# Retention attention into a SwiGLU block: the first pair in blocks of 128 tokens, SyncE asking for the weights, and the last half rounding moved

## The chip, the cores and the metric

The kernel runs on one core of a Trainium2 chip. The metric is the device time of one execution in microseconds (us). Three runs of the kernel before have a median of 1016.34 us (1016.2 to 1020.21). The profile is of one further execution, which took 1014.62 us in all, with a recorded span of 1012.9 us.

## The reference

Retention attention over q, k and v (8 batches, 8 heads, 576 tokens, 64 wide, float32) feeds a feed-forward block on 4608 tokens of width 512. The weights come as float64: 512 x 1536 twice and 1536 x 512 once.

```
scores = scale * q @ k.T
ret    = scores * where(i >= j, gamma[head] ** (i - j), 0)
x      = (ret @ v), heads side by side          # 4608 x 512
g      = x @ w_gate
out    = (silu(g) * (x @ w_val)) @ w_out
```

## The kernel before, in words

**Attention.** Two heads of one batch are a pair; a batch has four pairs (HP = 4), and there are 32. A pair is worked in chunks of 64 tokens. q and k are turned so that the 64 features lie on partitions; TensorE makes the scores of each chunk with itself (`scores`), which are multiplied by a decay mask `near` (`masked`, `own`); the chunk's key-value sums (`new_states`) are chained into running states on VectorE (`pairs`, `odd`, `evens`); and the outputs are the chunk's own part (`own_values`) and the part from the states (`earlier_values`), added in one bank of PSUM and put into x by `to_x`. Keys are scaled by a column of the table `tab`, which is loaded from DRAM.

The pairs 0 to 3, the first 512 tokens, are special. They are turned by TensorE (`transposes`, L466) and copied out of PSUM; pairs 1 to 3 have q scaled by GpSimd beforehand (`scale_run`, L735), pair 0 has its output scaled on VectorE instead (L645). `tick(t, 0, HP)` does one step of this start: scores and states of pair t-1, values of pair t-2, transposes of pair t. Later pairs are turned by VectorE (L492).

**The feed-forward block.** The 4608 tokens go in tiles: a first of 512, then four of 1024. For the first tile, `up0(f, chunks)` makes one of 12 filters f of 128 columns: gate and value, each four chunks (one per pair of x) of 128x128 weights against 512 tokens, in two of the four banks A, B, C, E; then the silu on ScalarE (L856) and the product on VectorE (L857). `down0` multiplies by w_out afterwards. Filters 0 and 1 are begun with chunks 0 and 1 while pair 3 is still being worked (L853), and finished with chunks 2 and 3. Filter 2 and the gate of filter 3 are written as two halves of 256 tokens (L850).

**Weights.** They are loaded in 18 pieces of 1 MB (`load_w`; `order` gives the sequence, pieces 0 to 11 gate and value of two filters each, 12 to 17 w_out), into three raw slots that take turns and one extra for the piece with m = 3. Each piece is turned from float64 into float32 in two halves j: ScalarE splits the words (`split`, L389 and L390), VectorE puts them together (`rounding`, L406 and L407). The split of a piece's second half asks for the piece three places later, which needs the slot. Before, SP asks for the first five pieces and ScalarE's queue for the rest.

**Order.** The order on every engine is the order of the program text (`manual_schedule`); there is no scheduler. The list `plan` interleaves roundings (`round_until`), `up0`, `tick` and the loads of later pairs (`load`, `next_load`) for filters 2 to 11. SP issues the loads of pairs in program order; each DMA uses one of eight semaphores, so a DMA waits until the one eight before it has landed. `end_loads` issues small loads from GpSimd for the last 64 tokens of batch 0.

Of the kernel before, what the change touches and what calls it, by code (L numbers as in the profile page):

```python
# [17 lines left out]
ALU = mybir.AluOpType  # L18
# [4 lines left out]
def tables(gamma, scale, L):  # L23

    g, at = np.array(gamma), np.arange(L)
    lane = np.arange(2 * L)[:, None]
    both = lambda t: np.repeat(t, L, axis=0).reshape(-1, 2 * L, t.shape[1]).transpose(1, 0, 2).reshape(2 * L, -1)
    twice = lambda t: np.concatenate([t, t])
    half = [np.repeat(g.reshape(-1, 2), L, axis=1).T ** (lane % 32 + 32 * r) for r in range(2)]
    pieces = scale * np.stack(half, axis=2).reshape(2 * L, -1)
    runs = scale * (g[None, :, None] ** ((4 * lane[:, :, None] + np.arange(4)) % L)).reshape(2 * L, -1)
    parts = [twice((g[:, None] ** -at).T), twice((g[:, None] ** (L - at)).T),
             both(g[:, None] ** L), both(g[:, None] ** (2 * L)), pieces, runs, both(scale * g[:, None] ** at),
             both((scale * g[:, None] ** at).reshape(-1, 2, L)[:, ::-1].reshape(-1, L))]  # L40
    return np.concatenate(parts, axis=1).astype(np.float32)
# [90 lines left out]
def kernel(  # L132
# [32 lines left out]
    nc = tc.nc  # L165

    B, H, S, D = q.shape
# [79 lines left out]
    def scaled(i):  # L247

        return 0 < i < HP
# [4 lines left out]
    def load(i):  # L254
# [6 lines left out]
        if i < HP:  # L261
# [11 lines left out]
            for h in heads:  # L273
                queues[i % 2].dma_start(out=blocks(t)[:, h % 2], in_=v[b, h, 0:CW].rearrange("(c p) d -> p c d", p=P))
# [35 lines left out]
    NCOL = 6 * H + 4 * HP  # L310
    nc.sync.dma_start(out=tab[:, 0:NCOL], in_=decays[:, 0:NCOL])
    load(0)
    load(1)
    ident = const.tile([P, P], F32, name="ident")
    make_identity(nc, ident)
    nc.scalar.activation(out=io[:, 0:1], in_=ident[:, 0:1], func=AF.Silu)
    inv, key = tab[:, 0:H], tab[:, H : 2 * H]
    step = tab[:, 2 * H : 2 * H + 2 * HP]
    piece = tab[:, 2 * H + 2 * HP : 2 * H + 4 * HP]
    run = tab[:, 2 * H + 4 * HP : NCOL]  # L320
# [11 lines left out]
    even_heads, odd_heads = slice(0, H, 2), slice(1, H, 2)  # L332
    for rows in half:
        decay(slice(0, H), slice(0, H), rows)

    load(2)
    nc.sync.dma_start(out=tab[:, NCOL:], in_=decays[:, NCOL:])
    load(3)
# [13 lines left out]
    order = [0, 1, 2, 3, 4, 5, 6, 12, 7, 8, 13, 9, 10, 14, 11, 15, 16, 17]  # L352
# [6 lines left out]
    def load_w(m, parts=range(2)):  # L359

        i, queue = order[m], nc.sync if m < 5 else nc.scalar
        n = m - (m > RAWS)
        raw = rest[:, raw_at + n % RAWS * 2048 : raw_at + (n % RAWS + 1) * 2048].rearrange("p (c x) -> p c x", c=HP)
        if m == RAWS:
            raw = x_odd[:, :, TW // 2 :]
        raws[i] = raw.bitcast(I32)
        dst, src = raw.bitcast(I64), weights[i][0]
        if i < NUP:
            for cols in [ts(2 * f + n, D) for f in parts for n in range(2)] if m <= RAWS else [slice(0, 2 * P)]:
                queue.dma_start(out=dst[:, :, cols], in_=src[:, :, cols])  # L370
        else:
            queue.dma_start(out=dst.rearrange("p (f c) n -> p f (c n)", f=2), in_=src)
# [7 lines left out]
    def split(j):  # L380

        i, f = halves[j]
        bits = bits_of(i, f)
        top, ulp = [rest[:, part_at + 512 * (2 * n + j % 2) : part_at + 512 * (2 * n + j % 2 + 1)] for n in range(2)]
        blocks = lambda a: a.rearrange("p (c m) -> p c m", m=P)
        nc.scalar.activation(out=blocks(top), in_=bits[:, :, :, 1].bitcast(F32), func=AF.Prelu, scale=2.0 ** -112, alpha=2.0 ** 32)  # L389
        nc.scalar.activation(out=blocks(ulp.bitcast(I32)), in_=bits[:, :, :, 0].bitcast(U32), func=AF.Copy, scale=2.0 ** -29)  # L390
        parts[j] = top.bitcast(I32), ulp.bitcast(I32)
        m = j - 2 if 1 < j < 4 else j // 2
        if f and m != RAWS and m + RAWS + (m < RAWS) < len(order):
            if j == 3:
                held.append(lambda: load_w(m + RAWS + (m < RAWS)))
            else:
                load_w(m + RAWS + (m < RAWS))
# [13 lines left out]
    for f in range(2):  # L411
        for m in range(2):
            load_w(m, (f,))
# [30 lines left out]
    def vector(i):  # L444

        return i == 0

    def transposes(i):
# [6 lines left out]
        copy = nc.scalar.copy if i else nc.vector.tensor_copy  # L455
        if i < HP:

            mine = (bankC, bankE) if i + 1 == HP else (bankB, bankA)
            parts = [(kT, kn, mine[0]), (qT, qk, mine[1])]
            if i == 0:  # L460
                parts.reverse()

            def turn(t, src, bank):
                for c in range(NFULL):
                    to = bank[:, c : 4 * P : NFULL] if t is qT and scaled(i) else bank[:, ts(c, P)]
                    nc.tensor.transpose(to, src[:, ts(c, P)], ident)  # L466

            def put(t, _, bank):
                if i or t is qT:
                    copy(t[:, 0:CW], bank)  # L470
                else:
                    copy(t[:, 0 : CW // 2], bank[:, 0 : CW // 2])
                    nc.scalar.copy(t[:, CW // 2 : CW], bank[:, CW // 2 :])

            if i + 1 == HP:
                for part in parts:
                    turn(*part)
                pieces = [lambda part=part: put(*part) for part in parts]
            else:
                for part in parts:  # L480
                    turn(*part)
                    put(*part)
# [13 lines left out]
        def keys():  # L496
# [5 lines left out]
            for hl, rows, at in parts:  # L502
                scale = key[rows, 2 * p + hl : 2 * p + hl + 1]
                if vector(i) or 1 < i < HP:
                    (nc.vector if vector(i) else nc.gpsimd).tensor_scalar(out=at, in0=at, scalar1=scale, scalar2=None, op0=ALU.mult)
                else:
                    nc.scalar.activation(out=at, in_=at, func=AF.Copy, scale=scale)
# [3 lines left out]
        return [keys] + pieces  # L511
# [64 lines left out]
    def masked(i):  # L576
# [6 lines left out]
        def copies():  # L583
            (nc.vector.tensor_copy if vector(i + 1) else nc.scalar.copy)(out=even, in_=z[:, 0])
# [151 lines left out]

    def tick(t, lo=HP, hi=NP, spread=False, then=None):
        go_on(len(pieces))
        if hi == HP:

            def new_pair():
                scores(t - 1, True)
                new_states(t - 1)
                pieces.extend(masked(t - 1))
                go_on(3)

            scale_run(t + 1)
            if lo < t < hi:
                new_pair()
            if lo <= t - 2 < hi:  # L750
                own_values(t - 2)
            for f in transposes(t) if lo <= t < hi and t + 1 < HP else ():
                f()
            if lo <= t - 2 < hi:
                earlier_values(t - 2)
                if t == HP:
                    up0(0, range(2))
                to_x(t - 2)[0]()
            if t + 1 == HP:
                split(0)  # L760
                after = transposes(t)
                rounding(0)
                for f in after:
                    f()
            if t == HP:
                rounding(2)
                rounding(3, False)
                new_pair()
                while held:
                    held.pop()()  # L770
                split(4)
                up0(1, range(2))
            return
# [68 lines left out]
    def up0(f, chunks):  # L842

        pair = banks[2 * (f % 2) : 2 * (f % 2) + 2]
        for gv, bank in enumerate(pair):
            for c in chunks:
# [6 lines left out]
                nc.tensor.matmul(bank, w, xs[0][:, c, :], start=(c == 0), stop=(c == HP - 1))  # L853
# [573 lines left out]
    for t in range(HP + 2):  # L1427
        tick(t, 0, HP)

        if t == 3:  # L1430
            load(HP)
        for j in {3: (1,), 5: (4, 5)}.get(t, ()):
            rounding(j)
    for c in range(2, HP):
        for f in range(2):
            up0(f, [c])
    load(HP + 1)
    for to, heads in ((even_heads, odd_heads), (odd_heads, even_heads)):
        decay(heads, to, half[1])
    nc.gpsimd.tensor_copy(out=last_near, in_=near[:, even_heads])  # L1440
    end_loads()
# [16 lines left out]
    plan.insert(1, lambda: tick(HP, HP, FIRST))  # L1458
    tick_at = {2: 4, 3: 5, 5: 6, 7: 7, 10: 8, 11: 9}
    for f in range(2, NF):  # L1460
        round_until({4: 12, 6: 13, 8: 14, 9: 15, 10: 16, 11: 17}.get(f, f + 2))
        plan.append(lambda f=f: up0(f, range(HP)))
        if f + 2 == NF:
            plan.append(lambda: split(2 * len(order) - 2))
# [3 lines left out]
        if f - 1 in tick_at and f < 7:  # L1468
            plan.append(lambda t=tick_at[f - 1]: next_load(t))
# [101 lines left out]
```

## Time and profile before

| what | value |
|---|---|
| median of three runs | 1016.34 us (1016.2 to 1020.21) |
| the profiled execution's own time | 1014.62 us |
| its span | 1012.9 us |
| TensorE busy | 1001.2 us, 99% of the span |
| VectorE, ScalarE, GpSimd busy | 714.8, 286.6, 561.9 us |
| moved by DMA | 194.38 MB, 192 GB/s on average |
| first matmul of filter 0, of filter 2 (timeline) | 24.02 us, 40.96 us |
| first matmul of `down0` (timeline) | 121.81 us |

A busy share is an average over the whole span. The change touches only the part before about 125 us, so the timeline and the busy time of short stretches say more about it. Starts are microseconds from the span's start. A float32 matmul appears as two records (two passes), so x32 is sixteen matmuls. Where an engine was idle before a row, the bracket at its end gives the time and what ended it.

### The profile page before, as it was taken

How to read it: one execution, taken by the hardware profiler on the slowest of the kernel's cores; microseconds unless marked ns; L12 is line 12 of the kernel's file. 1: busy time of each engine (PE TensorE's matmuls, PEld its weight loads, DVE VectorE, ACT ScalarE, POOL GpSimd, SP SyncE). 2: the span in 40 equal slices, each digit the busy share in tenths (PEclk: the TensorE clock that was granted, in tenths of full speed). 3: DMA queues.
4: the chain of work that ended last, by engine and by line, in shares of the span. 5: the costliest groups of instructions: out<-in, count | busy, mean ns of one | idle time of the engine just before them, and what ended most of it. 6: DMA issues, size and time to landing. Idle time of an engine off the chain costs nothing.

```text
span 1012.9 us, 21320 instructions
## 1 busy us (share of the span) xinstructions
PE 1001.2 (99%) x8336; PEld 825.6 (82%) x8336; DVE 714.8 (71%) x1206; ACT 286.6 (28%) x636; POOL 561.9 (55%) x589
## 2 busy tenths in 40 slices
PE   6999999999999999999999999999999999999998
PEld 5655555888888888888888888888888888888887
DVE  4488888677875766977777678866575767566645
ACT  4475522132423312132422202233220012232110
POOL 3400358979475228575564157746672586566614
PEclk9999999999999999999999999999999999999999
DMA  9999976877587786757577776434454554445553
GB/s 243 261 274 264 206 230 229 236 221 213 142 235 204 221 234 205 186 154 200 179 202 206 197 180 218 154 133 159 161 173 141 154 189 147 148 156 180 181 159 102
DMA packets 278892, 194.38 MB, mean 192 GB/s; under 512 B 212552, under 2 KB 246088, under 8 KB 278792
## 3 DMA queue, kind: packets, MB, share of 16 engines
q1 hardware_dynamic: 251464, 94.70, 36.5%
q10 hardware_dynamic: 26688, 97.92, 29.4%
q8 instruction: 66, 1.08, 0.5%
q0 software_dynamic: 640, 0.39, 0.2%
q14 instruction: 34, 0.28, 0.1%
HBM read 154.04 MB, written 38.93 MB: 191 GB/s over the span
## 4 chain that ended last, share of the span: by engine, by line
PE 96%; DVE 2%; DMA 1%; SPq 0%; ACT 0%; issue 0%; ACTq 0%; DVEq 0%
PE bankB L1186 12%; PE bankC L1186 12%; PE bankA L1186 11%; PE bankE L1186 11%; PE bankB L1392 7%; PE bankE L1392 7%; PE bankC L1392 7%; PE bankA L1392 6%; PE outer L532 2%; PE bankE L853 2%; PE bankA L853 2%; PE inner L1186 2%; PE outer L1186 2%; PE bankB L853 2%; PE outer L559 2%; PE bankC L853 2%
## 5 line engine op out<-in xcount | busy, mean ns | idle before, releaser
L1042 POOL TENSOR_TENSOR rest<-rest 128x512 f32<-128x512 f32 (+1 forms) x139 | 148.0, 1076 | 160.1 <-DVE rest L1042 112.7
L1201 POOL TENSOR_TENSOR arena<-rest,io 128x256 f32<-128x256 f32 x168 | 123.9, 750 | 88.9 <-ACT io L1200 84.2
L1200 ACT ACTIVATE io<-rest 128x256 f32<-128x256 f32 x192 | 79.3, 417 | 200.2 <-DVE rest L1042 132.5
L1186 PE MATMUL bankB<-rest,arena 128*128 128x256 f32 x448 | 114.6, 380 | 0.0
L1042 DVE TENSOR_TENSOR rest<-bankB,rest 128x512 f32<-128x512 f32 x116 | 78.5, 685 | 41.2 <-PE bankB L1186 28.5
L1186 PE MATMUL bankC<-rest,arena 128*128 128x256 f32 x416 | 106.3, 380 | 0.0
L1186 PE MATMUL bankA<-rest,arena 128*128 128x256 f32 x412 | 104.8, 379 | 0.0
L1042 DVE TENSOR_TENSOR rest<-bankA,rest 128x512 f32<-128x512 f32 x111 | 75.2, 685 | 39.3 <-PE bankA L1186 19.4
L1042 DVE TENSOR_TENSOR rest<-bankC,rest 128x512 f32<-128x512 f32 x110 | 74.5, 684 | 38.1 <-PE bankC L1186 25.6
L1042 DVE TENSOR_TENSOR rest<-bankE,rest 128x512 f32<-128x512 f32 x106 | 71.8, 685 | 35.7 <-PE bankE L1186 20.6
L1186 PE MATMUL bankE<-rest,arena 128*128 128x256 f32 x372 | 94.9, 380 | 0.0
L1186 PEld LDWEIGHTS bankB<-rest,arena 128*128 128x128 f32 x448 | 84.6, 190 | 12.2 <-DVE rest L1042 0.6
L1186 PEld LDWEIGHTS bankC<-rest,arena 128*128 128x128 f32 x416 | 78.5, 190 | 11.4 <-DVE rest L1042 0.8
L1186 PEld LDWEIGHTS bankA<-rest,arena 128*128 128x128 f32 x412 | 78.1, 190 | 10.9 <-DVE rest L1042 0.2
L1186 PEld LDWEIGHTS bankE<-rest,arena 128*128 128x128 f32 x372 | 70.3, 190 | 10.1 <-DVE rest L1042 0.6
L1042 POOL TENSOR_TENSOR arena<-arena 128x256 f32<-128x256 f32 (+1 forms) x76 | 70.2, 947 | 9.3 <-PE bankC L1186 7.9
L886 POOL TENSOR_TENSOR rest<-rest 128x512 f32<-128x512 f32 x21 | 29.1, 1408 | 73.4 <-DVE rest L407 58.2
L1392 PE MATMUL bankB<-arena 128*128 128x256 f32 x264 | 61.0, 381 | 0.0
L1392 PE MATMUL bankE<-arena 128*128 128x256 f32 x264 | 60.8, 380 | 0.0
L1392 PEld LDWEIGHTS bankE<-arena 128*128 128x128 f32 x264 | 50.0, 190 | 6.9
L1392 PEld LDWEIGHTS bankB<-arena 128*128 128x128 f32 x264 | 49.8, 190 | 6.9
L1392 PE MATMUL bankC<-arena 128*128 128x256 f32 x240 | 55.2, 379 | 0.0
(270 smaller groups left out, 1879.3 us busy)
## 6 DMA issues: line engine op xcount, KB each, us to landing
arena<-up ACTq DMA_DIRECT2D x63, 896.0 KB, 4.7
arena<-dn ACTq DMA_DIRECT2D x65, 384.0 KB, 3.2
arena<-dn SPq DMA_DIRECT2D x39, 384.0 KB, 3.2
out_dram<-rest SPq DMA_DIRECT2D x31, 256.0 KB, 3.0
qk<-in_q_dram SPq DMA_DIRECT2D x108, 72.0 KB, 3.7
qk<-in_k_dram SPq DMA_DIRECT2D x108, 72.0 KB, 3.5
dn<-rest SPq DMA_DIRECT2D x26, 256.0 KB, 2.8
up<-arena SPq DMA_DIRECT2D x13, 512.0 KB, 6.1
```

Source lines behind the costliest of these rows:

```text
L532: m = nc.tensor.matmul(value(i, hl, c), s["v"][rows, at], ret[rows, c % 2 if whole(i) else hl, c // 2], start=start, stop=start, skip_grou ...
L559: nc.tensor.matmul(xr[half[hl]] if c + 1 == NC else value(i, hl, c), state[half[hl], c, :], s["qT"][half[hl], ts(c, L)], start=False, stop ...
L853: nc.tensor.matmul(bank, w, xs[0][:, c, :], start=(c == 0), stop=(c == HP - 1))
L886: eng.tensor_tensor(out=dst, in0=srcs[0], in1=srcs[1], op=ALU.add if op[0] == "add" else ALU.subtract)
L1042: eng.tensor_tensor(out=out, in0=a, in1=b, op=ALU.add if sign > 0 else ALU.subtract)
L1186: m = nc.tensor.matmul(b[:, g * TB : (g + 1) * TB], w[:, g], x, start=(opens and g == 0), stop=True, skip_group_check=True)
L1200: nc.scalar.activation(out=s, in_=src[:, 0:TB], func=AF.Silu)
L1201: (nc.vector if busy and o != 2 and qd + 1 < NQ else nc.gpsimd).tensor_tensor(out=hid[:, qd, 2 * H + h, 2 * T + t], in0=src[:, TB : 2 * TB ...
L1392: nc.tensor.matmul(b[:, m * TB : (m + 1) * TB], lhs[:, qd, ts(m, P)], w[:, qd], start=(opens and qd == 0 and m == 0), stop=(qd == NQ - 1), ...
```

## The change

It has several parts, all in the part before the first `down0`.

- Pair 0 gets functions of its own. `first_scores` turns q and k, multiplies q by a table while copying it out of PSUM, scales the keys, and makes scores in blocks of 128 tokens, masked by a mask of 128x128 (`first_near`); `first_states`, `first_own` and `first_out` do the rest in blocks of 128. The table has 132 columns more in its first part.
- Matmuls of the identity whose result nobody reads are put on TensorE: eight before the transposes of pair 0's q, as far as they go, more between and behind its transposes, and 22 of 64x64 ahead of the first `up0`.
- The `tick` steps of pairs 0 to 3 are written out, with other places for the splits, roundings and the parts of `up0(0)` and `up0(1)`. All four pairs use banks C and E for their transposes. Values of a pair are loaded behind q and k of the first two pairs.
- SP asks for all pieces of weight but the one with m = 5, which stays with ScalarE's queue. The order of the pieces brings those of filters 6 to 9 before the first of w_out. The first halves of pieces 0 and 1 are asked for ahead of pair 3, and piece 4 ahead of `load(HP)`. Pieces 2 and 3 are loaded in one DMA instead of four.
- GpSimd waits for the last matmul of `up0(1)` before `end_loads`. The table's second part is loaded behind `load(HP)`; pair 4's transposes on VectorE go behind filter 2's product.
- The last half rounding (j = 35) goes behind the product of the last filter.

The diff, cut to its core:

```diff
-             for h in heads:
-                 queues[i % 2].dma_start(out=blocks(t)[:, h % 2], in_=v[...])
+                 if i == 0 and queue is nc.sync:
+                     nc.sync.dma_start(out=tab[:, 0:NCOL], in_=decays[:, 0:NCOL])
+             def values():
+                 for h in heads:
+                     queues[i % 2].dma_start(out=blocks(t)[:, h % 2], in_=v[...])
+             loaded[i] = (qk, kn, t)
+             return values
...
-     nc.sync.dma_start(out=tab[:, 0:NCOL], in_=decays[:, 0:NCOL])
-     load(0)
-     load(1)
+     values = [load(0), load(1)]
...
+     for f in values:
+         f()
+     load(2)()
...
+     nc.gpsimd.affine_select(out=first_near.rearrange("p (h i) -> p h i", i=P), ...)
...
-     order = [0, 1, 2, 3, 4, 5, 6, 12, 7, 8, 13, 9, 10, 14, 11, 15, 16, 17]
+     order = [0, 1, 2, 3, 4, 5, 6, 7, 8, 9, 12, 10, 11, 13, 14, 15, 16, 17]
...
-         i, queue = order[m], nc.sync if m < 5 else nc.scalar
+         i, queue = order[m], nc.scalar if m == 5 else nc.sync
...
-     for f in range(2):
-         for m in range(2):
-             load_w(m, (f,))
+     for m in range(2):
+         load_w(m, (0,))
+     load(3)()
+     for m in range(2):
+         load_w(m, (1,))
      load_w(2)
      load_w(3)
...
+     def first_scores():
...
+         for _ in range(2):
+             nc.tensor.matmul(bankB[0:D, 0:D], ident[0:D, 0:D], ident[0:D, 0:D], start=True, stop=True)
+         for src, bank, idle in ((None, None, 6), (qk, bankE, 2), (kn, bankC, 1)):
+             for c in range(NFULL if bank else 0):
+                 nc.tensor.transpose(bank[:, ts(c, P)], src[:, ts(c, P)], ident)
+             for _ in range(idle):
+                 nc.tensor.matmul(bankB[:, 0:P], ident, ident, start=True, stop=True)
+         nc.vector.tensor_tensor(out=blocks(qT), in0=blocks(bankE), in1=table(first_qry), op=ALU.mult)
+         nc.vector.tensor_copy(kT[:, 0 : CW // 2], bankC[:, 0 : CW // 2])
+         nc.scalar.copy(kT[:, CW // 2 : CW], bankC[:, CW // 2 :])
...
+         for c, hl in first:
+             nc.tensor.matmul(inner[:, hl, ts(c, P)], kT[half[hl], ts(c, P)], qT[half[hl], ts(c, P)], ...)
+         for hl in range(2):
+             nc.vector.tensor_tensor(out=first_ret[:, hl], in0=blocks(inner[:, hl]), in1=table(first_near[:, ts(hl, P)]), op=ALU.mult)
...
-     for t in range(HP + 2):
-         tick(t, 0, HP)
...
+     scale_run(1)
+     first_scores()
+     scale_run(2)
+     turn_pair(1)
+     first_states()
+     first_own()
+     new_pair(1)
+     turn_pair(2)
+     first_out()
+     split(0)
+     rounding(0, False)
+     scale_run(3)
+     new_pair(2)
+     own_values(1)
+     split(1)
+     for _ in range(22):
+         nc.tensor.matmul(bankB[0:D, 0:D], ident[0:D, 0:D], ident[0:D, 0:D], start=True, stop=True)
+     up0(0, [0], [0])
+     earlier_values(1)
+     to_x(1)[0]()
+     put = transposes(3)
+     rounding(1, False)
+     for f in put:
+         f()
+     up0(0, [1], [0])
+     up0(0, [0], [1])
+     split(2)
+     own_values(2)
+     earlier_values(2)
+     up0(0, [1], [1])
+     to_x(2)[0]()
+     rounding(2)
+     rounding(3, False)
+     new_pair(3)
+     load(HP)
+     nc.sync.dma_start(out=tab[:, NCOL:], in_=decays[:, NCOL:])
+     split(4)
+     up0(1, range(2))
+     own_values(3)
+     earlier_values(3)
+     to_x(3)[0]()
...
+     wait = nc.gpsimd.nop()
+     tc.add_manual_dep(wait.ins, last_up[0].ins.name, ...)
      end_loads()
...
-         round_until({4: 12, 6: 13, 8: 14, 9: 15, 10: 16, 11: 17}.get(f, f + 2))
+         if f == 3:
+             plan.append(lambda: tick(HP, HP, FIRST))
+         round_until({4: 7, 5: 8, 6: 12, 7: 10, 8: 13, 9: 15, 10: 16, 11: 17}.get(f, f + 2))
+         last_half = plan.pop() if f + 1 == NF else None
          plan.append(lambda f=f: up0(f, range(HP)))
+         if last_half:
+             plan.append(last_half)
...
-         if f - 1 in tick_at and f < 7:
-             plan.append(lambda t=tick_at[f - 1]: next_load(t))
+         if f in (3, 5, 6):
+             plan.append(lambda t={3: 4, 5: 5, 6: 6}[f]: next_load(t))
```

## The prediction

> **What bounds the kernel now.** I read the page first, then the busy time by stage, then the timeline of the first 45 us, then the DMA view of two stretches. On the page, TensorE is busy 99% of the span and holds the chain that ended last:
>
> ```profile
> span 1012.9 us, 21320 instructions
> PE 1001.2 (99%) x8336; PEld 825.6 (82%) x8336; DVE 714.8 (71%) x1206; ACT 286.6 (28%) x636; POOL 561.9 (55%) x589
> ...
> PE 96%; DVE 2%; DMA 1%; SPq 0%; ACT 0%; issue 0%; ACTq 0%; DVEq 0%
> ```
>
> So only time before TensorE becomes gapless can be won. The stage view (columns: stretch, its length, then busy us and records of PE, PEld, DVE, ACT, POOL, then clock, DMA share, GB/s) shows where that is:
>
> ```profile
> 0.00:10.00 10.00, 4.36 (x73) 3.43 (x74) 1.64 (x4) 2.02 (x4) 3.21 (x11) 1.00 0.94 202
> 10.00:20.00 10.00, 8.97 (x236) 7.71 (x235) 6.46 (x16) 4.11 (x9) 3.96 (x4) 1.00 1.17 270
> 20.00:30.00 10.00, 8.99 (x171) 5.77 (x172) 7.27 (x15) 8.12 (x17) 1.97 (x2) 1.00 1.02 283
> 30.00:40.00 10.00, 9.82 (x80) 4.68 (x80) 4.68 (x11) 5.30 (x10) 7.56 (x15) 1.00 1.03 246
> ```
>
> 7.9 us are idle before 40 us; DMA is at its limit throughout. TensorE's timeline shows a second loss, slow work, and the marks that I measure against (start, length, work):
>
> ```profile
> 12.49 1.13 PE L573 MATMUL inner<-rest,kT 64*64 64x64 f32 x32 [0.72 <-ACT rest L470]
> ...
> 15.26 1.11 PE L466 MATMUL bankB<-ident,rest 128*128 128x128 f32 x4
> 16.16 1.06 PE L466 MATMUL bankA<-ident,rest 128*128 128x128 f32 x4
> 17.15 0.68 PE L559 MATMUL outer<-rest,state 64*64 64x64 f32 x28
> 17.94 0.69 PE L573 MATMUL inner<-rest,kT 64*64 64x64 f32 x32
> ...
> 20.63 0.66 PE L466 MATMUL bankC<-ident,rest 128*128 128x128 f32 x4
> ...
> 24.02 1.98 PE L853 MATMUL bankA<-rest,arena 128*128 128x512 f32 x4
> ...
> 33.99 1.12 PE L853 MATMUL bankA<-rest,arena 128*128 128x512 f32 x2
> ...
> 40.96 3.62 PE L850 MATMUL bankA<-rest,arena 128*128 128x256 f32 x16
> ```
>
> Until 17 us work runs slowly although the granted clock is shown as 1.00: 32 records of 64x64 (16 matmuls of two passes) take 0.90 us to the next group's start at 13.39, then 0.52 (17.94 to 18.46); four transposes take 0.90 (15.26 to 16.16), then 0.49 (20.63 to 21.12). The first projection matmul starts at 24.02, its last two chunks at 33.99, the third filter (f = 2) at 40.96. From 40.96 TensorE has no gap to the end of the first stage. **The change is worth what it moves 40.96.**
>
> **The first pair.** Before, q of pair 0 was second in SP's list and landed at 4.47. Now it is first on both queues (0.4 us earlier, 4.1); the table (98 KB instead of 32 KB) follows k, about 6.1 by its place behind 0.5 MB (the first 4 us moved 0.49 MB, the next two 0.53). Eight idle matmuls of one identity start when it is ready (1.5 us). A 128-wide matmul is two passes of 0.9/4 us, so six take 2.7 and two small ones 0.2: TensorE is occupied to 4.4. Transposes of q end at 5.5, two idle ones fill to 6.3, k's transposes end at 7.3. I take the clock as full from 8 us. VectorE then multiplies q by its table (0.69) and copies half of k (0.42) to 7.8; ScalarE's half (0.37) ends at 8.2. Its table load of 1.28, which the page shows at 5.62, now waits for a later DMA, about 6.5, and still ends before.
>
> The 8 scores of 128x128, two at a time, cost 4 x 0.25 = 1.0 (8.8). Pair 1's transposes cost 2 x 0.49 (9.8); GpSimd has one mask more, 0.43 as the other 256-wide ones, ahead of scaling pair 1's q, which ends at 9.0, behind the cover of k's transposes. States (0.45), own values (0.9), pair 1's scores and states (0.52 + 0.6) reach 12.3; the masks of 2 x 0.69 end at 10.2, before own values need them. Pair 2's k is the next doubt: 2.2 MB lie ahead up to it, and the stages give 2.0 MB by 10 us and 2.5 by 12, so with its landing 12.2. Transposes end at 13.3, the first outputs (6 of 128) at 13.9; scores wait for ScalarE's copies (two of 0.59, to 14.1); states and pair 1's own values end at 16.0. The three table multiplies of the old output path (1.29 on VectorE) become one copy of 0.59 on ScalarE.
>
> **The 22 idle matmuls.** The trace does not show them. All use one quarter of the array. If they ran four abreast like the 64x64 row, 22 x 0.52/16 = 0.7 us; one after another, with half a 128-wide pass each, 22 x 2 x 0.061 = 2.7. I take 2.7, the nearer row since they share one place: 18.7. The first weight half is ready at 17.2 (asked for near 10.5 instead of 13.42, 5.1 us to land, 1.24 for ScalarE's two, 0.69 for the last of VectorE's): it hides behind them, and without them it would be the wait.
>
> **From there to f = 2.** Two filters' first halves are 8 matmuls of 0.86 = 6.9; pair 1's earlier values 0.6; pair 3's transposes 1.0; pair 2's own and earlier values 1.3; pair 3's scores and states 1.2; its own and earlier values 1.35; waits for ScalarE's copies of pair 1 (1.13) 0.2: 12.55, to 31.25. The fourth weight half (5.4 MB, landed near 23) is rounded by 27, under the gate's matmuls. Then 6.97, as from 33.99 to 40.96: f = 2 at 38.2, **2.8 us earlier**. With the idle run at its lower bound the same list gives 36.3, 4.7 earlier.
>
> **Weights on SP's queue.** Only weight 5 stays with ScalarE. SP now asks for weight 4 before load(4), weights 6 to 8 behind load(5), 9 to 11 behind load(6), 12 and 13 behind load(7), 14 behind load(8), 15 to 17 behind load(9). So these weights queue behind every wait of the loads: buffers released by TensorE or VectorE, and the landing of the eighth DMA before. In before one such wait was long:
>
> ```profile
> SPq L287 <- DMA rest<-in_moe_w_out_dram: 7.3, 1, 7.3
> ```
>
> The DMA view of 42 to 60 us (loads and weights on two queues) and of 112.5 to 128 (loads alone, on SP) gives the prices:
>
> ```profile
> DMA packets 9333, 4.45 MB, mean 247 GB/s; under 512 B 8030, under 2 KB 8157, under 8 KB 9331
> ...
> DMA packets 14586, 2.46 MB, mean 159 GB/s; under 512 B 14582, under 2 KB 14582, under 8 KB 14582
> ```
>
> A load alone takes 7.4 us (issues at 113.01 and 120.58) at about 0.85 of the DMA engines; 1.05 MB of weight alone about 2.9 (at 370 GB/s, where the first stretch was fastest). In a row from 19 us on: weight 4 lands near 33, load(5) ends near 50, weights 6 to 8 near 59, 9 to 11 near 75, 12 and 13 near 88, 15 near 110. Their roundings stand ahead of the silu products of filters 4, 6, 8, 9 on VectorE, which TensorE needs at about 72, 89, 103 and 113 (their times before, less 2.8). All are met, the last with 1 us or less. I charge 0, with an upper bound in rival D. By the Trainium skill, "DMA: Bandwidth & Descriptors", section "Issuing engines are not separate DMA queues", DMAs from several engines share the same 16 DMA engines and a second issuer saves only issue time; by that alone the move costs nothing and D has no price. The two rows disagree in part: SP by itself did not fill the engines.
>
> **The rest.** Pair 4's VectorE transposes (0.77 + 0.73) go behind f = 2's product, needed only 10 us later. GpSimd's extra wait holds its small loads from 31.5 to 38; behind it are 20 issues of some 13 us, ending near 51, used near 60. The last half rounding (1.49 + 1.54 there) goes behind the last product: that product had been at 123.66, just before its bank's matmul at 124.49, so what it saves is a stall that earlier work would expose; 0 now.
>
> **Sum.** 1012.9 - 2.8 = 1010.1 of span, 1014.62 - 2.8 = 1011.8 of the profiled execution's own time. The median of the runs lies 1.7 above that execution; taken off it, 1016.34 - 2.8 = **1013.5**.
>
> **Rivals.**
> A, the forecast: 2 to 4.7 us won, 1011.6 to 1014.3. Chance 0.46.
> B, more is won: the idle run is short (4.7), and before's typical run also lost its 1.7 us in the slow start, which the early idle work now avoids: up to 6.4, 1009.9. For it: the slow groups end only at 17; against: nothing shows that the 1.7 lies there. 0.28.
> C, the slow state lasts: if the groups from 8 to 14 us run as before 17, they cost 1.0 + 0.8 + 0.45 + 0.9 less what copies hide, about 2.8: 1016.3. For it: TensorE ran unbroken from 7.79 to 11.77 and stayed slow. Against: it became fast after 12.49 to 17 with only small gaps, and the new run from 1.5 is longer. The Trainium skill, "TensorE: Matmul & The Clock Gate", Part 4, says transposes do not engage the full clock; that would make 1016.3, but the trace turned fast right behind eight transposes. 0.13.
> D, SP's queue is late: weights behind load(5) to load(9) land too late, VectorE's in-order roundings hold the products of filters 8 and 9, and TensorE stalls for a bank near 103 to 113. It decides once a weight takes over 3.2 us behind a load of 7.4. At 4.0, twelve weights from 6 on land 13 us later: less about 3 of slack, 10 lost, 7 net, 1023.3. Against: the same bytes had landed by 109.9 before. 0.13.
>
> **Numbers.** About 0.5% (5.1 us) is what a measurement of this kernel can tell from no change. Faster by more: nearly all of B, 0.25; slower by more: most of D, 0.11; the rest 0.64. The range runs from B's end, 1009.9, over C, 1016.3, into D's mild end, 1017.5, leaving out some 0.15, most of D and of what lies past B.
>
> **What would show it.** Right: 64x64 groups at 0.52 by 9 us, the first 512-wide matmul near 18.7, f = 2 near 38, no TensorE gap to 118. Wrong: cold groups beyond 10 us; a wait of the filters 8 to 11 for a bank, with ScalarE's splits waiting for a weight DMA; SP waiting long inside load(5).

## The result, and the profile after

The changed kernel is slower: 1029.26 us (median of 4 runs, 1028.49 to 1032.05) beside 1016.27 for the kernel before on the same chip (4 runs), a ratio of 1.0124 with a 95% interval of 1.0093 to 1.0155. Forecast was 1013.5, range 1009.9 to 1017.5: time and range are wrong, and so is the side. The profiled execution of the changed kernel took 1032.05 us with a span of 1030.3, 17.4 more than before. Lines of the new code stand lower: the projection matmuls are L871 and L868, silu L874, product L875, split L398 and L399, rounding L415 and L416, requests for weights L379 and L381, for pair loads L290 and L295, `down0` L882.

The page of the changed kernel, the lines that answer to those shown of before:

```profile
span 1030.3 us, 21317 instructions
PE 1009.4 (98%) x8338; PEld 830.5 (81%) x8338; DVE 709.9 (69%) x1203; ACT 285.1 (28%) x636; POOL 561.5 (55%) x590
...
PE 90%; DMA 4%; SPq 2%; ACT 2%; issue 1%; DVE 1%; POOL 0%; ACTq 0%; POOLq 0%
```

The chain that ended last was 96% TensorE and 1% DMA; now DMA, SP's queue and ScalarE hold 8% of it, some 80 us. TensorE's timeline (start, length, work, idle time before and its releaser) shows where that bites:

```profile
16.40 2.73 PE L1461 MATMUL bankB<-ident 64*64 64x64 f32 x44
19.06 1.12 PE L871 MATMUL bankA<-rest,arena 128*128 128x512 f32 x2
...
39.57 3.62 PE L868 MATMUL bankA<-rest,arena 128*128 128x256 f32 x16
...
71.78 3.70 PE L871 MATMUL bankA<-rest,arena 128*128 128x512 f32 x8 [0.47 <-ACT io L874]
80.37 3.70 PE L871 MATMUL bankC<-rest,arena 128*128 128x512 f32 x8 [1.45 <-ACT io L874]
91.62 3.70 PE L871 MATMUL bankA<-rest,arena 128*128 128x512 f32 x8 [1.04 <-ACT io L874]
...
114.93 5.93 PE L871 MATMUL bankA<-rest,arena 128*128 128x512 f32 x8 [9.32 <-ACT io L874]
...
136.78 1.13 PE L882 MATMUL bankA<-rest,arena 128*128 128x512 f32 x2
```

Against before, filter 2 (39.57) is 1.4 us early and `down0` (136.78) is 15.0 late: 16.4 us are lost between the two. 12.3 of them are the waits in brackets, all for a silu (0.4 more at filter 11), 9.3 in one piece ahead of filter 10. Another 2.2 are that filter's first bank, 5.93 instead of 3.70: the stage view shows a granted clock of 0.53 there. The rest are pieces of 0.1 to 0.5. (2.4 more are lost behind 136.78, 1.5 of them in one wait that the profile can't name. This execution is the longest of the four.) Before, filter 10 followed filter 9 without a wait:

```profile
103.27 3.60 PE L853 MATMUL bankA<-rest,arena 128*128 128x512 f32 x8
```

What the silu waits for is in the chain of waits on ScalarE (engine, work and releaser: us in total, times, longest), from 40 to 140 us:

```profile
ACT rest L398 <- DMA rest<-in_moe_w_out_dram: 12.4, 2, 6.7
ACT rest L398 <- DMA rest<-in_moe_w_gate_dram: 12.3, 1, 12.3
ACT rest L398 <- DMA rest<-in_moe_w_val_dram: 8.8, 2, 5.8
```

ScalarE stands 33.5 us in front of splits whose weight has not landed. Ahead of filter 10 it is the split of weight 14, and behind that split stands the silu that frees bank A:

```profile
113.19 0.66 ACT L398 ACTIVATE rest<-rest 128x512 f32<-128x512 f32 x1 [5.73 <-DMA rest<-in_moe_w_out_dram]
...
114.29 0.59 ACT L874 ACTIVATE io<-bankA 128x512 f32<-128x512 f32 x1
```

SP's own timeline shows why it has not (L290: requests of a pair load; L379, L381: of weights, which I number by their place m in the order):

```profile
50.99 1.40 SPq L379 DMA_DIRECT2D rest<-in_moe_w_gate_dram  x1
...
53.59 10.63 SPq L290 DMA_DIRECT2D qk<-in_q_dram  x4
...
69.70 0.73 SPq L379 DMA_DIRECT2D rest<-in_moe_w_val_dram  x1
...
73.34 10.07 SPq L290 DMA_DIRECT2D qk<-in_q_dram  x4
...
87.58 0.73 SPq L379 DMA_DIRECT2D rest<-in_moe_w_val_dram  x1
...
103.56 1.49 SPq L381 DMA_DIRECT2D rest<-in_moe_w_out_dram  x1
...
115.84 2.15 SPq L381 DMA_DIRECT2D rest<-in_moe_w_out_dram  x3
```

Behind three weights, four requests of a pair load take over 10 us, and the next weight is asked for only behind the whole load. Weight 14 is asked for at 103.56 and weights 15 to 17 from 115.84; before, ScalarE had asked for the one in place 14 at 85.38 and for the last at 101.94:

```profile
85.38 0.39 ACTq L370 DMA_DIRECT2D rest<-in_moe_w_val_dram  x1
...
101.94 0.37 ACTq L372 DMA_DIRECT2D rest<-in_moe_w_out_dram  x1
```

The stage view (columns as in the prediction) shows the DMA engines less than full meanwhile, where before they had 1.12, 1.03 and 1.07 from 80 to 110 us:

```profile
80.00:90.00 10.00, 9.63 (x159) 5.53 (x163) 9.16 (x23) 5.18 (x11) 0.00 (x0) 1.00 0.80 156
90.00:100.00 10.00, 8.96 (x55) 4.28 (x50) 6.60 (x14) 6.64 (x13) 0.00 (x0) 1.00 0.92 244
100.00:110.00 10.00, 5.62 (x14) 2.16 (x12) 8.45 (x21) 2.47 (x4) 0.00 (x0) 0.96 0.82 194
110.00:120.00 10.00, 5.07 (x7) 2.25 (x8) 2.75 (x5) 2.81 (x5) 0.00 (x0) 0.53 0.78 167
```

### The profile page after: what moved, and what is told of

It is laid out like the page before. It is cut to its first block, busy times and chain, and to the rows that moved or that the text cites. A ratio compares the mean times of both kernels' runs of the same rounds, so it can differ in the third digit from the quotient of the medians.

```text
span 1030.3 us, 21317 instructions
## 1 busy us (share of the span) xinstructions
PE 1009.4 (98%) x8338; PEld 830.5 (81%) x8338; DVE 709.9 (69%) x1203; ACT 285.1 (28%) x636; POOL 561.5 (55%) x590
## 4 chain that ended last, share of the span: by engine, by line
PE 90%; DMA 4%; SPq 2%; ACT 2%; issue 1%; DVE 1%; POOL 0%; ACTq 0%; POOLq 0%
PE bankB L1204 12%; PE bankC L1204 12%; PE bankA L1204 12%; PE bankE L1204 11%; PE bankB L1410 7%; PE bankE L1410 7%; PE bankC L1410 7%; PE bankA L1410 6%; DMA rest<-in_moe_w_out_dram 2%; PE inner L1204 2%; PE outer L1204 2%; PE outer L517 2%; PE outer L544 1%; PE inner L558 1%; PE inner L528 1%
## 5 line engine op out<-in xcount | busy, mean ns | idle before, releaser
L1204 PE MATMUL bankB<-rest,arena 128*128 128x256 f32 x448 | 114.6, 380 | 0.1
L1204 PE MATMUL bankC<-rest,arena 128*128 128x256 f32 x416 | 106.4, 380 | 0.2 <-DVE rest L1060 0.2
L1204 PE MATMUL bankA<-rest,arena 128*128 128x256 f32 x412 | 104.9, 379 | 0.0
L1204 PE MATMUL bankE<-rest,arena 128*128 128x256 f32 x372 | 94.9, 380 | 0.0
L1204 PEld LDWEIGHTS bankB<-rest,arena 128*128 128x128 f32 x448 | 84.6, 190 | 12.3 <-DVE rest L1060 0.7
L1204 PEld LDWEIGHTS bankC<-rest,arena 128*128 128x128 f32 x416 | 78.5, 190 | 12.0 <-DVE rest L1060 1.4
L1204 PEld LDWEIGHTS bankA<-rest,arena 128*128 128x128 f32 x412 | 78.0, 190 | 11.3 <-issue 0.4
L1204 PEld LDWEIGHTS bankE<-rest,arena 128*128 128x128 f32 x372 | 70.3, 190 | 10.1 <-DVE rest L1060 0.6
L1060 POOL TENSOR_TENSOR arena<-arena 128x256 f32<-128x256 f32 (+1 forms) x76 | 70.1, 945 | 10.6 <-PE bankC L1204 9.0
```

The lines of the kernel that those rows point to most:

```text
L1060: eng.tensor_tensor(out=out, in0=a, in1=b, op=ALU.add if sign > 0 else ALU.subtract)
L1204: m = nc.tensor.matmul(b[:, g * TB : (g + 1) * TB], w[:, g], x, start=(opens and g == 0), stop=True, skip_group_check=True)
```

## The experiments

The theory after this reading: weights wait in SP's line behind pair loads; because the split of the next weight stands ahead of a silu on ScalarE, the silu waits with it, and TensorE for the silu's bank. Rivals: the new order of pieces and places, the later pair loads, the new start. Ratios are to the kernel before on the same chip, with 95% intervals.

**Only the queue put back.**

```diff
-         i, queue = order[m], nc.scalar if m == 5 else nc.sync
+         i, queue = order[m], nc.sync if m < 5 else nc.scalar
```

> The changed kernel with one line put back: weights 6 to 17 are asked for by ScalarE again; start, order of pieces, places and idle matmuls stay as changed. Theory (the pieces wait in SP's queue behind the pair loads): no wait of TensorE for ScalarE's silu from filter 2 to the first down projection; filter 2 starts near 39.6 as in the changed kernel, down projection near 120.4, time 1013 to 1016.5, which is the kernel before less 1.4 or a little better. Rival (the new order of pieces, the later loads or the new start cost the time): filters 7 to 11 late as before this edit, 1026 to 1031.

Measured 1016.54 (12 runs, 1013.23 to 1018.74), ratio 1.0008 (0.9995 to 1.0021). In its timeline no wait for a silu is left:

```profile
39.86 3.62 PE L868 MATMUL bankA<-rest,arena 128*128 128x256 f32 x16
...
102.32 3.70 PE L871 MATMUL bankA<-rest,arena 128*128 128x512 f32 x8
...
120.96 1.13 PE L882 MATMUL bankA<-rest,arena 128*128 128x512 f32 x2
```

ScalarE asks for weight 9 at 64.69 (SP: 69.70), 14 at 87.08 (103.56) and 17 at 103.44. So the loss is the queue's, and of the rivals nothing over the interval is left. But nothing is won either, although in this profile filter 2 starts 1.1 us earlier than before and the execution took 1013.89 us in all, 0.7 less than the profiled one before.

**Only the queue changed, in the kernel before.**

```diff
-         i, queue = order[m], nc.sync if m < 5 else nc.scalar
+         i, queue = order[m], nc.scalar if m == 5 else nc.sync
```

> The kernel before with only the queue changed: weights 4 and 6 to 17 on SP, weight 5 on ScalarE, all else as before. Theory: the same pieces wait behind the same pair loads, TensorE stalls for the silu at filters 7 to 11, 1022 to 1034. Rival (the queue alone is harmless, the new order and places do it): 1015 to 1018.

Measured 1028.50, ratio 1.0132 (1.0112 to 1.0152): the whole loss from that line alone. The profile is of its longest execution (1031.26), in which filter 2 comes only at 42.53 after a wait of 2.00 us at 22.72, ahead of the first weight that the line moves. The long wait is at the same filter:

```profile
111.75 5.59 PE L853 MATMUL bankA<-rest,arena 128*128 128x512 f32 x8 [5.42 <-ACT io L856]
```

**Before's order and places, weights on SP.**

```diff
-     order = [0, 1, 2, 3, 4, 5, 6, 7, 8, 9, 12, 10, 11, 13, 14, 15, 16, 17]
+     order = [0, 1, 2, 3, 4, 5, 6, 12, 7, 8, 13, 9, 10, 14, 11, 15, 16, 17]
...
-         round_until({4: 7, 5: 8, 6: 12, 7: 10, 8: 13, 9: 15, 10: 16, 11: 17}.get(f, f + 2))
+         round_until({4: 12, 6: 13, 8: 14, 9: 15, 10: 16, 11: 17}.get(f, f + 2))
```

> The changed kernel with the order of pieces and the places of the roundings of the kernel before, weights still on SP. Theory (the queue is the cause, the order moves only which filter stalls): 1022 to 1036. Rival (the new order and places cause the loss): 1013 to 1018.

Measured 1025.51, ratio 1.0103 (1.0080 to 1.0127): still slow, filter 10 waiting 5.55 us.

**The next split behind the silu.** Each `up0` now stands ahead of the split of the next weight in program order (`behind` is the last half rounded ahead of it; the half behind that goes into the list `behind_up`); requests and VectorE's roundings keep their places.

```diff
-             plan.extend(lambda j=j: rounding(j, j != 2 * len(order) - 3) for j in (2 * m, 2 * m + 1))
+             while behind_up:
+                 plan.append(lambda j=behind_up.pop(): split(j))
+             behind = 2 * m + 1 if not todo or order.index(i) < todo[0] else -1
+             if behind > 0:
+                 behind_up.append(behind + 1)
+             plan.extend(lambda j=j, b=behind: rounding(j, j != b) for j in (2 * m, 2 * m + 1))
...
          plan.append(lambda f=f: up0(f, range(HP)))
...
-         if f + 2 == NF:
-             plan.append(lambda: split(2 * len(order) - 2))
+         while behind_up:
+             j = behind_up.pop()
+             if j < len(halves):
+                 plan.append(lambda j=j: split(j))
```

> The changed kernel, weights still on SP, but ScalarE splits the next piece behind the silu of the filter instead of ahead of it; roundings on VectorE stay where they were. Theory (the silu of filter 8 waits on in-order ScalarE for one piece more than it has to): filter 10 starts near 105 instead of 114.9, a part of the wait returns at filter 11 through the products that still stand behind VectorE's roundings; 1018 to 1025. Rival (VectorE's order alone holds the banks, ScalarE's place is indifferent): 1028 to 1031.

Measured 1025.16, ratio 1.0092 (1.0073 to 1.0111), just over the upper end of what the theory gave. That is some 4 us less than the changed kernel, but the two intervals overlap. Filter 10 starts at 103.89, and the wait comes back whole at filter 11:

```profile
103.89 3.70 PE L871 MATMUL bankA<-rest,arena 128*128 128x512 f32 x8 [1.51 <-ACT io L874]
...
123.22 6.06 PE L871 MATMUL bankC<-rest,arena 128*128 128x512 f32 x8 [9.94 <-ACT io L874]
```

So filter 8's silu did wait for a weight that it had no use for; but its place mostly decides which filter pays for weights that are late. Part of the expectation failed: I had looked to VectorE for the rest of the wait, and it is ScalarE again, with the splits of weight 15 ahead of the silu of filter 9.

**Only weights 12 to 17 back on ScalarE.**

```diff
-         i, queue = order[m], nc.scalar if m == 5 else nc.sync
+         i, queue = order[m], nc.scalar if m == 5 or m > 11 else nc.sync
```

> The changed kernel with only weights 12 to 17 given back to ScalarE; 4 and 6 to 11 stay on SP. Theory (delay adds up load by load, and the stall at filter 10 is that of weights 13 and 14 behind loads 7 and 8): the waits of 0.5, 1.5 and 1.0 us at filters 6 to 8 stay, the 9.3 us at filter 10 and the slow 2.2 us behind it go; 1015 to 1020. Rival (the early weights' delay alone carries through to filter 10): over 1024.

Measured 1017.05, ratio 1.0019 (1.0011 to 1.0028). The delay adds up: with the last six weights off SP's queue, 2 us are left of the loss. The places were only half right: 1.6 us at filter 8, 1.7 at filter 10, none at 6 and 7.

**Pair loads 6 to 9 on GpSimd's queue, weights on SP.**

```diff
-         queue = nc.sync
+         queue = nc.gpsimd if 5 < i < 10 else nc.sync
```

> The changed kernel with weights still on SP, but the pair loads 6 to 9 are asked for by GpSimd, which has nothing to do from 60 to 100 us; no data less is moved. Theory (the weights wait in SP's queue behind the pair loads' own waits, not because SP asks for them or because the bytes share the DMA engines): weights 9 to 17 are asked for when their buffer is free, the 9.3 us wait at filter 10 is gone, 1013 to 1018. Rival (the DMA engines are shared and full, whichever queue asks): 1024 to 1030, as the changed kernel.

Measured 1026.75 (1021.13 to 1027.54), ratio 1.0103 (1.0082 to 1.0124): against the theory. Weight 8 is asked for at 51.97 and lands only at 75, when its split starts; behind that split stands the silu for which filter 6 waits (ScalarE's and TensorE's timeline):

```profile
75.07 0.66 ACT L398 ACTIVATE rest<-rest 128x512 f32<-128x512 f32 x1 [5.06 <-DMA rest<-in_moe_w_gate_dram]
```

```profile
76.82 5.86 PE L871 MATMUL bankA<-rest,arena 128*128 128x512 f32 x8 [5.62 <-ACT io L874]
```

GpSimd asked for loads 6 and 7 from 53.15 to 78.4; with the weights' queue alone put back, SP does so from 59.82 to 87.8. So two loads ran beside weights 6 to 9. Weights 6 and 7 were asked for late, behind load 5 on SP (50.22 and 51.41, beside 39.38 and 44.41 with their queue put back); weight 8 was not (51.97 beside 53.25), and yet it took 23 us to land. Here a second queue was no shelter from loads that ran at the same time. The run changes two things, place in line and time of the loads, so it does not by itself decide for either. In the two that follow, first the weights leave SP's line and the loads stay, then all stay on SP and two loads come later.

**Weights 6 to 17 on GpSimd's queue, loads on SP.**

```diff
-         i, queue = order[m], nc.scalar if m == 5 else nc.sync
+         i, queue = order[m], nc.sync if m < 5 else nc.scalar if m == 5 else nc.gpsimd
```

> The changed kernel with weights 6 to 17 asked for by GpSimd instead of SP; the pair loads stay on SP where they are. Theory (weights wait in line behind pair loads; any second queue frees them): weight 9 is asked for near 65 instead of 69.7, weight 14 near 88 instead of 103.6, no wait over 2 us at filter 10, 1014 to 1019. Rival (it is ScalarE's asking that matters, or the DMA engines are simply full): 1024 to 1030.

Measured 1015.92, ratio 1.0005 (0.9989 to 1.0020), no wait for a silu from filter 2 on. Weight 9 is asked for at 58.90 and weight 14 at 86.77. So it need not be ScalarE that asks: either other queue frees the weights.

**All on SP, pair loads 8 and 9 asked for later.**

```diff
-         if f in (3, 5, 6):
-             plan.append(lambda t={3: 4, 5: 5, 6: 6}[f]: next_load(t))
+         if f in (3, 5, 8, 9):
+             plan.append(lambda t={3: 4, 5: 5, 8: 6, 9: 7}[f]: next_load(t))
...
-         if f in (7, 10):
-             if f == 10:
-                 plan.append(lambda: next_load(9))
+         if f == 10:
+             plan.append(lambda: next_load(9))
              plan.append(lambda t=tick_at[f]: next_load(t))
```

> The changed kernel with all weights on SP, but pair loads 8 and 9 asked for behind filters 8 and 9 instead of 6 and 7, so that weights 14 and up stand ahead of them in the same queue. Theory (what counts is how many loads stand ahead of a weight): weight 14 is asked for near 93 instead of 103.6, the 9.3 us wait at filter 10 with its 2.2 us of slow clock is gone or under 2 us, the 3 us lost at filters 6 to 8 stay, 1016 to 1021, unless VectorE's transposes of pair 8 then wait for their load. Rival (SP's queue as such is slow for weights): 1026 to 1031.

Measured 1020.61, ratio 1.0059 (1.0037 to 1.0082): over half of the loss is gone without a second queue, only by asking for loads 8 and 9 behind weights 14 to 16. Filter 10 waits 2.67 us instead of 9.32, a little over the 2 that I gave. The 3 us at filters 6 to 8, which I left standing, are 0.2; they were 0 and 0.5 in the two profiles above with the split moved and with before's order, but 1.25 with only the queue changed in the kernel before and 1.6 with weights 6 to 11 on SP. So they come in some executions and not in others, and one profile of each run cannot size them.

**Loads 6 to 9 in long packets, all on SP.** q and k are read in the wrong layout, as said.

```diff
                  for a in range(P // SQ):
+                     if 5 < i < 10:
+                         queue.dma_start(out=qk[a * SQ : (a + 1) * SQ, n].rearrange("t j d -> t (j d)"),
+                                         in_=src[b, 2 * p + a // 2, (a % 2) * (S // 2) : (a % 2 + 1) * (S // 2)].rearrange("(t j) d -> t (j d)", t=SQ))
+                         continue
                      queue.dma_start(
```

> The changed kernel with all weights still on SP; q and k of the pair loads 6 to 9 are read as whole rows, 2304 bytes in one piece instead of 18 pieces of 128 bytes: same bytes, same places, same waits for buffers, but not the values that belong there. Theory (what keeps the weights back is the time that the small packets of a load take on the queue): loads 6 to 9 shrink from 14 to 16 us to under 8 each, filter 10 does not wait, 1014 to 1019. Rival (SP's waits for buffers inside a load keep them back): loads stay above 12 us and the time above 1024.

Measured 1022.68, ratio 1.0063 (1.0045 to 1.0080), between theory and rival. From first request to last, loads 6 to 9 take 13.4, 11.1, 8.5 and 7.9 us instead of 15.6, 14.1, 13.1 and 10.6, together 12.5 less. Filter 10 waits 1.5 and filter 11 2.62. By the ratios about half of the loss is gone (0.63% instead of 1.24%, both with wide intervals), so the small packets are a good part of it and not all. What is left shows in SP's waits: 20.6 us in the requests of these loads are put down to weights that have yet to land, those just ahead in the line.

**The 22 idle matmuls, with the queue put back.**

```diff
-     for _ in range(22):
-         nc.tensor.matmul(bankB[0:D, 0:D], ident[0:D, 0:D], ident[0:D, 0:D], start=True, stop=True)
```

> The changed kernel with weights 6 to 17 on ScalarE again and without the 22 small idle matmuls ahead of the first projection matmul. The prediction said that these hide behind the landing and rounding of the first weight half. Theory as predicted: the first projection matmul starts within 0.7 us of the 19.35 that it has with them, and the time is 1013 to 1017, the same. Rival: the 2.7 us are in the way, it starts at 16.9 and the time is about 2.5 less; third: the stop slows TensorE's next matmuls, 1 to 2 us more.

Measured 1020.79, ratio 1.0054 (1.0042 to 1.0066). The first projection matmul starts at 18.43 instead of 19.35, held by a rounding: the weight hid 1.7 of the 2.7 us of idle matmuls, not all. Yet the kernel is 4 us slower, which none of the three expectations had. Its profile shows 1.19 us at filter 10, 1.0 at L1204 for a DMA, and two waits with no releaser: 1.55 at 123.03 and 1.75 at 621.08. Behind the last one TensorE ran slowly:

```profile
621.08 0.50 PE L558 MATMUL inner<-qT,kT 64*64 64x64 f32 x17 [1.75 <-issue]
621.50 1.98 PE L1204 MATMUL bankC<-rest,arena 128*128 128x256 f32 x4
```

The next four records start 1.78 us later and those behind them 1.71, where 0.86 is usual here, and the granted clock is 0.50 from 622 to 624. So some 3.5 us of this one execution are lost half a millisecond behind the edit. Whether they come from it is not shown, and why all five executions took over 1019 us stays open.

**The early idle matmuls, with the queue put back.**

```diff
-         for src, bank, idle in ((None, None, 6), (qk, bankE, 2), (kn, bankC, 1)):
+         for src, bank, idle in ((qk, bankE, 0), (kn, bankC, 0)):
```

> The changed kernel with weights 6 to 17 on ScalarE again and without the nine 128-wide idle matmuls of the first 7 us; the two small ones and the 22 later ones stay. Prediction: without an early run the groups of the first pair run at half speed to about 13 us, 2 to 3 us later at the 22 idle matmuls, less what the landing of the first weight hides: 1015 to 1019. Rival (TensorE waits for data there anyway and its clock is of no account): 1013 to 1016.5, no difference.

Measured 1023.46 (1022.85 to 1024.02), ratio 1.0068 (1.0046 to 1.0091). The timeline shows the slow start:

```profile
6.72 1.23 PE L747 MATMUL inner<-rest,kT 64*128 64x128 f32 x8 [0.52 <-DVE kT L741]
...
9.38 1.11 PE L466 MATMUL bankC<-ident,kn 128*128 128x128 f32 x4
...
42.77 3.62 PE L868 MATMUL bankA<-rest,arena 128*128 128x256 f32 x16
...
78.47 6.54 PE L871 MATMUL bankA<-rest,arena 128*128 128x512 f32 x8 [4.13 <-ACT rest L398]
```

Transposes take 1.11 us at 9.38 (0.66 with the idle matmuls), and full speed comes by 13.3. Filter 2 is 2.9 us late. Of these, 1.9 are there when the slow work ends (pair 1's scores start at 13.34 instead of 11.45); the other 1.1 are a longer wait at 19.14, for which the profile names no releaser. A wait of 4.13 us at 78.47 and 2.8 of slow matmuls behind it come on top. That wait goes back to a pair load, not to a weight: k, asked for at 67.24, lands 9.31 us later, and its scaling on ScalarE stands ahead of the split that the profile names as what ended the wait. Slower than both expectations: without the nine idle matmuls the kernel takes 6 (by the ratios) to 7 us (1023.46 beside 1016.54) more, and the slow start is under a third of that.

**The last half rounding, with the queue put back.**

```diff
-         last_half = plan.pop() if f + 1 == NF else None
+         last_half = None
```

> The changed kernel with weights 6 to 17 on ScalarE again and the last half rounding back ahead of the last product. The prediction charged the move at 0 us. As predicted: within 1 us of the kernel with the queue alone put back, 1014 to 1018. Rival: the product is late for its bank by the 1.5 us of the rounding, and the down projection waits, 1 to 1.5 us more.

Measured 1016.89, ratio 1.0004 (0.9989 to 1.0018), no difference. The stall that the move takes away does show, where the prediction placed it:

```profile
124.60 1.13 PE L882 MATMUL bankE<-rest,arena 128*128 128x512 f32 x2 [0.65 <-DVE arena L875]
```

**Queue, order and places put back.** Both edits above (queue of the first run, order and places of the third).

> The changed kernel with weights 6 to 17 on ScalarE and also the order of pieces and places of the roundings of the kernel before. What is left of the change is the start, the idle matmuls, the later pair loads and the last half rounding. Theory: order and places are worth nothing once TensorE has no gap, 1013 to 1017, within 1 us of the kernel with the queue alone put back (1016.5). Rival: the new order costs in the runs above 1016; then this one is 1 to 2 us less.

Measured 1018.13, ratio 1.0030 (1.0017 to 1.0042), 1.6 us above the kernel with the queue alone put back (2.2 by the ratios). Its profile has waits of 0.56 us at filter 8 and 1.67 at filter 10. So the new order does not cost; it may be worth a little (the intervals just overlap), where I had said nothing.

**Queue put back and the split behind the silu.** The edits of the first and the fourth run together.

> The changed kernel with weights 6 to 17 on ScalarE again and, beside it, the split of the next piece behind the silu of the filter. With the queue alone put back the profiled execution gained 0.7 us and the median nothing (1016.5 beside 1015.4), with runs up to 1018.7. Theory (in those runs late pieces hold the silu of filters 6 and 8 for 1 to 2 us): 1013 to 1015.5, with the long runs gone. Rival (the long runs come from elsewhere, or the later split makes the roundings late): 1015.5 to 1018.

Measured 1015.46 (12 runs, 1012.58 to 1017.21), ratio 0.9988 (0.9973 to 1.0004): the best of all, and still not to be told from the kernel before. It lies where theory and rival meet (1015.5), so it decides for neither. No version here beats the kernel before.

## Why the prediction was wrong, step by step

**The start** went nearly as forecast. k's transposes are at full speed at 6.6 us (I had taken 8), the idle run took 2.66 us (2.7), the first projection matmul came at 19.06 (18.7). The list behind it was mis-sized: 13.54 us to 32.60, not 12.55. So filter 2 won 1.4 us, not 2.8; rival A's mechanism at half its size. And one profile each is thin: with the same new start filter 2 comes between 39.34 and 40.59 in the profiles here, and with the old one at 40.96 or at 42.53. Rival C is refuted by its own mark. Its price of 2.8 is met by the 2.9 of leaving out the early idle matmuls, but partly by luck: only 1.9 of them are slow work. That the 22 later ones hide behind the weight held for 1.7 of 2.7 us.

**"Weights on SP's queue ... I charge 0"** is the step that failed. The mechanism was named in rival D, with a chance of 0.13; its price there, 1023.3, was 6 us short. Three terms of it:

- The serial sum. I gave 7.4 us to a load and 2.9 to a weight, as each runs alone. Loads 6 to 9 with the nine weights 6 to 14 would be 4 x 7.4 + 9 x 2.9 = 55.7 us; from weight 6's request (50.99) to weight 15's (115.84) it took 64.85, 9.2 more. Weight 15, forecast to land near 110, was split at 122.66. In one line each delays the other: from 40 to 125 us a q request of a pair load lands 9.1 us (median) after it is asked for, and 5.2 with the queue alone put back. The load's own time is not all of it: loads shorter by 12.5 us (long packets) left about half of the loss.
- The landing. I put a weight's landing 2.9 us behind its request. Weight 14 took 9.54 (103.56 to 113.10), beside what was asked for just ahead of it (load 8) and just behind it (load 9). But a slow landing is not what the one queue brought: the pieces of w_out land in 10.0 us here (median), in 8.6 with the queue alone put back, and in 9.4 on GpSimd's queue, which lost nothing. What differs is when they are asked for.
- The need. I counted roundings ahead of the products on VectorE. What stopped TensorE was the silu on ScalarE, which alone frees banks A and C, and ahead of it the split of one weight more. Moving it gave 4 us by the medians (1025.16 beside 1029.26), with intervals that overlap; that the wait moves to filter 11 is plain in the profile.

Together these ate the slack that I had called "1 us or less", and behind the idle 9.3 us the slow clock (0.53) cost 2.2 more. I had read that SP by itself did not fill the engines (0.85) and still weighed it as free.

The Trainium skill, "DMA: Bandwidth & Descriptors", section "Issuing engines are not separate DMA queues", says that a second issuing engine saves only the time to initiate, which is usually small. It is not small here: the same bytes, asked for by GpSimd or ScalarE instead of SP, save 13 us, since a weight that stands in line behind pair loads is asked for up to 16 us later, and with one queue the engines fall to a share of 0.78 to 0.92. The measurement decides against that page's rule where megabytes and small packets share one queue.

**The rest** (GpSimd's wait, the last half) cost nothing that can be measured, as charged.

**Where the start's gain went** once the queue is put back is only argued. The stretch from 40 to 120 us is full of DMA (share 0.88 to 1.24); the profiles of the near copies show waits of 0.2 to 1.7 us there or just behind it (0.2 and 0.65 with the last half rounding put back, 1.6 and 1.7 with weights 6 to 11 on SP, 0.7 with the split moved, 1.1 on GpSimd's queue), which the profile of before does not have. TensorE has no gap in that stretch before; so what comes earlier meets weights that do not. One more sign: 6 of the 12 executions with the queue alone put back have a mean granted clock under 1, as the slow stretches behind long waits give it, and 1 of 17 of the kernel before on the same chip. With GpSimd's queue it is 3 of 10 beside 4 of 13, so this proves nothing either.

## What to carry to other kernels

A request costs more than its bytes: ask what stands ahead of it in its queue, when that lands, and who holds the buffer that the next request needs. Where a queue is changed "at no cost", sum request by request to the landing of the last, with the measured landing beside other traffic and not the time of a transfer alone, and follow each late piece to the first in-order engine that stands in front of it. A slack of 1 us on a sum of 60 is no slack.

## What was not expected of the hardware

How long TensorE may wait before its clock falls can be bounded from these runs. Four matmuls of 128x512 (eight records) took 3.70 us behind waits of 0.2 to 1.68 us, 5.40 behind 2.62 and 2.67, and 5.10 to 6.54 behind 4.13 to 9.94. So the price, 1.4 to 2.8 us, hardly grows with the wait. Between these there is no sharp limit: the wait of 1.75 us at 621.08 without the 22 idle matmuls was followed by a granted clock of 0.50, and so was that of 2.00 at 22.72 in the kernel before with only the queue changed (0.50 from 24 to 26), but not that of 1.88 at 18.43 without the 22 (1.00). By the Trainium skill, "TensorE: Matmul & The Clock Gate", section "Why this matters for your kernels", it is gaps over about 3 us that throughput drops from; here waits of 1.75 to 2.67 us were enough. The granted clock shows such a fall (0.53 from 110 to 120 us of the changed kernel), but not the slow start, which is shown as 1.00.

When the slow start ends varies from one execution to the next: with the same instructions, transposes are slow until 17 us in the profile of before and fast from 9.90 in that of the kernel before with only the queue changed.

One 1 MB weight landed in anything from 6 us (median of the gate weights before) to 17.87 us (weight 9 with the pair loads on GpSimd's queue) and 23 (weight 8 there, by the start of its split), by what else was on the way.
